# A column of maxima to all partitions: by a TensorE matmul, or by a VectorE transpose and two transfers through memory

## The chip, the cores and the metric

The kernel runs on one core of a Trainium2 chip. A core has a matrix engine (TensorE, PE in the profile, with PEld for its weight loads), three engines for elementwise work (VectorE as DVE, ScalarE as ACT, GpSimd as POOL), a queue engine that issues transfers (SyncE, SP), and DMA engines that move data between device memory and the on-chip memory SBUF. Matmuls write to PSUM, a small memory of banks. The metric is the device time of one execution in microseconds; lower is better.

## The reference

The inputs are q, k and v of shape (8 batches, 8 heads, 576 positions, 64 channels) and four weights. First comes a linear attention: q goes through a softmax over its 64 channels, k through a softmax over the 576 positions, then

```python
kv  = np.einsum('bhsd,bhse->bhde', k_s, v)      # 64x64 per head
out = np.einsum('bhsd,bhde->bhse', q_s, kv)
```

The heads are laid side by side (x has shape 8, 576, 512), and an MLP mixer follows:

```python
h  = np.maximum(xt @ w_tok1, 0.0) @ w_tok2      # xt: x transposed, over the positions
u  = x + h.transpose(0, 2, 1)
h2 = np.maximum(u @ w_ch1, 0.0) @ w_ch2         # 512 -> 1536 -> 512
return u + h2
```

The softmax of k needs, for every channel, the maximum over all positions. The division by its sum is done later, on the rows of kv.

## The kernel before

The work on q, k and v is cut into 32 **units**, one for each batch and pair of heads (4 units a batch). A unit's k lies in SBUF as `k_t`, with positions on the 128 partitions and five blocks of 128 channels in the free dimension (5 x 128 positions, two heads of 64 channels). The same k also comes transposed as `kt_t`, with the 128 channels on the partitions and the positions in the free dimension, so that the maximum is a reduction along the free dimension.

Units 0 to 7 (the "early" ones, L221 to L231) exponentiate the transposed copy and turn it back on TensorE. Units 8 to 31 go another way, L233 to L238. Their maxima `mc` are a column (128 partitions x 1), but they have to be subtracted from `k_t`, where the channels lie in the free dimension. So all 128 maxima must stand in every partition:

- L219, VectorE: `mc` is the maximum over `kt_t`.
- L233, ScalarE: `dg` is the identity scaled by `mc` per partition, that is a diagonal of the maxima.
- L235, TensorE: a matmul of a matrix of ones with `dg` gives a PSUM bank in which every row holds all maxima.
- L236, ScalarE: that bank is copied to `mb` in SBUF.
- L237, GpSimd: `mb` is subtracted from `k_t`. L238, ScalarE: the exponential.

`dg` and `mb` are single buffers; `mc` has two; `kt_t` has one buffer for the later units and `k_t`, `q_t` have two.

What follows for a unit: `softmax_q` (L245 to L267, with the split of q into a high and a low part, the low part by GpSimd, L115), `stage_kv` (the matmuls of `k_t` with v, L277), `stage_y` (L337), `stage_qT` (transposes of q on VectorE, L315 and L323), `stage_h1` (L345) and `stage_u` (L381). Their PSUM banks come in turn from the four of the pool `ps_h`.

Around this runs the channel MLP as 108 **steps**, nine groups of 512 columns by twelve blocks of the hidden dimension. Step (g, f) does `ch1` (L409, twelve matmuls into a `ps_h` bank), then ScalarE and VectorE make `h2h` and `h2l` from it (L412, L413), and `ch2` (L421, twelve matmuls into four `ps_o` banks) consumes them; `ch2` of a step stands behind `ch1` of the next one in the program. Every third step takes the stages of one unit between its `ch1` and `ch2`, from the table `todo` that is written out by hand.

In that table the softmax of unit n+1 stands at the same step as the matmuls of unit n, and the loads of unit n+2 half a step later. All loads go through SP's queue: `kt_t`, `q_t` and `k_t` by L137, L140 and L144, v by L154 and L155. The results go out through ScalarE's queue (L454). Each engine and each queue works through its own instructions in order. That order, in which work of later units may stand ahead of earlier program text, is settled when the kernel is built, by a scheduler that works with estimated durations; on the chip it is fixed, and an instruction whose input is late holds up what is behind it on its engine.

Of the kernel before, what the change touches and what calls it, by code (L numbers as in the profile page):

```python
# [8 lines left out]
F32 = mybir.dt.float32  # L9
F32R = mybir.dt.float32r  # L10
U32 = mybir.dt.uint32
AF = mybir.ActivationFunctionType
# [3 lines left out]
P = 128  # L16
# [4 lines left out]
def attn_mixer_kernel(ctx: ExitStack, tc: tile.TileContext, q, k, kt, v, wt, out, dims):  # L21
# [3 lines left out]
    nc = tc.nc  # L25
    B, H, S, D, TOK, DM, DCH, wide = dims
    NJ = DM // P
# [8 lines left out]
    NE = 2 * NJ  # L36
# [6 lines left out]
    sm = ctx.enter_context(tc.tile_pool(name="sm", bufs=2))  # L43
# [6 lines left out]
    ident = const.tile([P, P], F32R, name="ident")  # L50
# [11 lines left out]
    ones = const.tile([P, P], F32, name="ones")  # L62
# [26 lines left out]
    dg = lay.tile([P, P], F32, name="dg")  # L89
    for i in range(3):  # L90
        slots[i][1] = lay.tile([P, NJ, CW], F32R, name=f"ul{i}")
    mb = lay.tile([P, P], F32, name="mb")
# [14 lines left out]
    Q = 32  # L107

    def f32(ap):
        return ap.bitcast(F32)  # L110
# [8 lines left out]
    def ps_unit(dtype=F32):  # L119

        pools = unit_banks[0]
        pool, name = pools[turn[0] % len(pools)]
        turn[0] += 1
        return pool.tile([P, 512], dtype, name=name)
# [87 lines left out]


    turned_k = []

    def softmax_k(u):
        ktt = u["kt"]
        mc = sm.tile([P, 1], F32, name="mc")
        nc.vector.tensor_reduce(mc, ktt, axis=AX.X, op=ALU.max)  # L219
        kx = u["k"]  # L220
        if u["early"]:  # L221
            nc.vector.tensor_scalar(mc, mc, -1.0, None, op0=ALU.mult)
            nc.scalar.activation(ktt, ktt, AF.Exp, bias=mc)
            t = ps_unit()
            for c in range(C):
                nc.tensor.transpose(t[:, c * P : (c + 1) * P], ktt[:, c * P : (c + 1) * P], f32(ident))
            nc.scalar.copy(kx[:, 0:C, :], t.rearrange("p (c d) -> p c d", c=C))
            t = ps_unit()
            turned_k.append(nc.tensor.transpose(t[:, 0:P], ktt[:, S0 : S0 + P], f32(ident)).ins)
            nc.scalar.copy(kx[:, C, :], t[:, 0:P])  # L230
            return  # L231

        nc.scalar.activation(dg, f32(ident), AF.Copy, scale=mc)  # L233
        t = ps_unit()
        nc.tensor.matmul(t[:, 0:P], ones, dg, start=True, stop=True)  # L235
        nc.scalar.copy(mb, t[:, 0:P])  # L236
        nc.gpsimd.tensor_tensor(kx, kx, mb.unsqueeze(1).broadcast_to([P, C1, P]), op=ALU.subtract)  # L237
        nc.scalar.activation(kx, kx, AF.Exp)  # L238

# [223 lines left out]
    def soft(n):  # L463
        if n < NU:
            softmax_k(units[n])
            softmax_q(units[n])
# [204 lines left out]
```

## Time and profile before

| | before |
|---|---|
| runs shown, median (lowest to highest) | 818.27 us (816.95 to 819.36) |
| the profiled execution's own time | 817.88 us |
| its span in the trace | 816.1 us |
| granted TensorE clock, mean | 0.992 of full speed |
| DVE busy, ACT busy, POOL busy | 486.7 us, 342.2 us, 83.6 us |
| instructions | 11997 |

The profile is one execution. The span runs from the first to the last recorded instruction; the time of the execution is 1.8 us longer than it. A matmul is recorded with its whole way through the array, so that the records of neighbouring matmuls overlap; how long one holds the array is read from the distance between their starts, or from the chain of work, in which each piece begins where the one before it ends. A 32-bit matmul of `ones` with `dg` leaves two records. Five line numbers serve for many tiles: L114 and L115 are the two instructions of the helper `split`.

### The profile page before, as it was taken

To read this page: it belongs to the slowest core of one execution; us is meant where nothing else is said; L and a number is where in the kernel's file an instruction comes from. 1 tells how busy PE (TensorE), PEld (TensorE's weight loads), DVE (VectorE), ACT (ScalarE), POOL (GpSimd) and SP (SyncE) were. 2 spreads that over 40 slices of the span, in tenths; PEclk is the share of its full clock that TensorE was granted. 3 is DMA by queue.
4 is the path that set the end of the run, shared out by engine and by line. 5 is a ranking of instruction groups with operands and counts; after the bars stand their busy time and mean duration, and the time that the engine had idled before them with its cause. 6 is when DMAs were issued, how large, how long until landed. Compare 5 with 4: busy or idle time off the path is not lost.

```text
span 816.1 us, 11997 instructions
## 1 busy us (share of the span) xinstructions
PE 797.1 (98%) x4512; PEld 677.0 (83%) x4512; DVE 486.7 (60%) x1104; ACT 342.2 (42%) x898; POOL 83.6 (10%) x69
## 2 busy tenths in 40 slices
PE   7799999989999999999999999999999999999997
PEld 5688888878888888888888888888888888888886
DVE  6999998887876555755576555755575314113112
ACT  6977564448553334343444444443443321101110
POOL 1000010102121100111111111111011100000200
PEclk8999999999999999999999999999999999999999
DMA  9752433414223111322232222312121001001001
GB/s 298 245 162 93 149 110 109 145 65 124 86 63 115 52 30 53 110 61 64 63 100 79 64 64 63 113 51 63 26 87 35 15 1 51 1 1 52 1 1 51
DMA packets 60633, 63.55 MB, mean 78 GB/s; under 512 B 40864, under 2 KB 40992, under 8 KB 60576
## 3 DMA queue, kind: packets, MB, share of 16 engines
q1 hardware_dynamic: 55392, 53.36, 21.8%
q10 hardware_dynamic: 5184, 9.44, 3.1%
q8 instruction: 35, 0.57, 0.3%
q14 instruction: 22, 0.18, 0.1%
HBM read 53.35 MB, written 9.44 MB: 77 GB/s over the span
## 4 chain that ended last, share of the span: by engine, by line
PE 89%; DVE 6%; DMA 3%; ACT 1%; issue 1%; DVEq 0%; ACTq 0%
PE ps_h L409 34%; PE ps_o L421 34%; PE ps_h L381 8%; PE ps_h L337 6%; PE ps_h L277 2%; DMA stg<-in_w 2%; PE ps_h L345 1%; PE ps_o L381 1%; DVE mc L219 1%; PE ps_h L235 1%; DVE cv_s L176 1%; DVE q_t L323 1%; DMA q_t<-in_q 1%; DVE st L245 1%; ACT q_t L251 1%
## 5 line engine op out<-in xcount | busy, mean ns | idle before, releaser
L409 PE MATMUL ps_h<-uh,cw 128*128 128x512 f32 x864 | 269.7, 392 | 0.6 <-DVE cw L115 0.6
L421 PE MATMUL ps_o<-h2h,cw 128*128 128x512 f32 x864 | 263.4, 394 | 2.2 <-DVE cw L115 2.2
L421 PEld LDWEIGHTS ps_o<-h2h,cw 128*128 128x128 f32 x864 | 160.6, 189 | 34.3 <-ACT h2h L412 2.4
L409 PEld LDWEIGHTS ps_h<-uh,cw 128*128 128x128 f32 x864 | 160.3, 188 | 33.2 <-DVE cw L115 1.0
L412 ACT ACTIVATE h2h<-ps_h 128x512 fp32r<-128x512 f32 x108 | 64.5, 597 | 292.8 <-PE ps_h L409 276.6
L413 DVE SCALAR_TENSOR_TENSOR h2l<-ps_h,h2h 128x512 fp32r<-128x512 f32 x108 | 74.0, 685 | 187.3 <-ACT h2h L412 186.9
L409 PE MATMUL ps_h<-ul,cw 128*128 128x512 f32 x432 | 168.2, 389 | 0.0
L421 PE MATMUL ps_o<-h2l,cw 128*128 128x512 f32 x432 | 161.7, 392 | 0.0
L421 PEld LDWEIGHTS ps_o<-h2l,cw 128*128 128x128 f32 x432 | 81.4, 189 | 16.8
L409 PEld LDWEIGHTS ps_h<-ul,cw 128*128 128x128 f32 x432 | 81.1, 188 | 17.0
L115 POOL TENSOR_TENSOR ql<-q_t,qh 128x640 fp32r<-128x640 f32 x24 | 39.3, 1636 | 484.8 <-ACT qh L114 406.3
L323 DVE COPY q_t<-cv_s 32x160 f32<-32x160 f32 (+1 forms) x264 | 65.8, 249 | 6.3 <-POOL ql L115 3.0
L245 DVE TENSOR_REDUCE st<-q_t 128x10 f32<-128x640 f32 x32 | 26.2, 818 | 41.8 <-DMA q_t<-in_q 41.8
L237 POOL TENSOR_TENSOR k_t<-k_t,mb 128x640 f32<-128x640 f32 x24 | 38.0, 1582 | 73.8 <-ACT mb L236 73.8
L323 ACT COPY q_t<-cv_s 32x128 f32<-32x128 f32 (+1 forms) x120 | 36.8, 307 | 2.1 <-DVE cv_s L315 0.7
L219 DVE TENSOR_REDUCE mc<-kt_t 128x1 f32<-128x640 f32 x32 | 26.0, 812 | 14.7 <-ACT dg L233 12.4
L381 PE MATMUL ps_h<-w2h,hh 128*128 128x320 f32 (+1 forms) x112 | 33.4, 299 | 0.0
L256 ACT ACTIVATE q_t<-q_t 128x640 f32<-128x640 f32 x24 | 17.8, 741 | 36.4 <-DVE q_t L255 36.4
L381 PE MATMUL ps_h<-w2l,hh 128*128 128x320 f32 (+1 forms) x112 | 33.0, 296 | 0.0
L381 PE MATMUL ps_h<-w2h,hl 128*128 128x320 f32 (+1 forms) x112 | 32.7, 298 | 0.0
L388 ACT CAST uh<-ps_h 128x320 fp32r<-128x320 f32 (+4 forms) x76 | 25.4, 336 | 15.1 <-PE ps_h L381 11.8
L389 DVE TENSOR_TENSOR ul<-ps_h,uh 128x320 fp32r<-128x320 f32 (+4 forms) x76 | 27.2, 373 | 4.0 <-ACT uh L388 3.1
(144 smaller groups left out, 1061.9 us busy)
## 6 DMA issues: line engine op xcount, KB each, us to landing
stg<-in_w SPq DMA_DIRECT2D x28, 512.0 KB, 4.1
kt_t<-in_kt SPq DMA_DIRECT2D x32, 320.0 KB, 3.1
q_t<-in_q SPq DMA_DIRECT2D x32, 320.0 KB, 3.3
v_t<-in_v SPq DMA_DIRECT2D x64, 128.0 KB, 2.8
out<-stg ACTq DMA_DIRECT2D x32, 256.0 KB, 2.1
k_t<-in_k SPq DMA_DIRECT2D x24, 320.0 KB, 3.5
v_t<-in_v SPq DMA_DIRECT2D x32, 32.0 KB, 2.7
out<-part ACTq DMA_DIRECT2D x4, 256.0 KB, 2.0
```

What stands on the lines that cost most here:

```text
L115: lo_eng.tensor_tensor(lo, src, f32(hi), op=ALU.subtract)
L219: nc.vector.tensor_reduce(mc, ktt, axis=AX.X, op=ALU.max)
L237: nc.gpsimd.tensor_tensor(kx, kx, mb.unsqueeze(1).broadcast_to([P, C1, P]), op=ALU.subtract)
L245: nc.vector.tensor_reduce(st[:, 0, :], qt, axis=AX.X, op=ALU.max)
L323: eng(qx[ys, 0:n, xs], turned[xs, 0:n, ys])
L337: nc.tensor.matmul(y[:, 0:TOK], a, w, start=(i == 0), stop=(i == len(mm) - 1))
L381: nc.tensor.matmul(t[:, 0:N], a, w, start=(i == 0), stop=(i == len(mm) - 1))
L389: nc.vector.tensor_tensor(ul, src, f32(uh), op=ALU.subtract).ins,
L409: nc.tensor.matmul(t, cw[f][x][:, n, :], w, start=(i == 0), stop=(i == 3 * NJ - 1))
L412: nc.scalar.activation(hh, t, AF.Relu).ins,
L413: nc.vector.scalar_tensor_tensor(hl, t, 0.0, f32(hh), op0=ALU.max, op1=ALU.subtract).ins,
L421: nc.tensor.matmul(o, cw[f][x][:, n, :], w, start=(first and i == 0), stop=(last and i == 2))
```

## The change

For the last twenty units (`u["n"] >= NE + NJ`, units 12 to 31), L233, L235 and L236 are replaced. The maximum goes straight into the first column of `dg`. One VectorE transpose of 32 x 32 blocks turns columns 0 to 31 of `dg` into columns 32 to 63, block by block: in partition 0, 32, 64 and 96 there then stands a row of 32 maxima. (Columns 1 to 31 hold older values, which land in other rows and aren't read.) One transfer on SP's queue brings the four rows to a tile `row` of 128 numbers in device memory, which has two buffers; a second transfer on the same queue reads it into all 128 partitions of `mb`. L237 and L238 stay as they are. Units 8 to 11 keep the matmul.

```diff
+    dram = ctx.enter_context(tc.tile_pool(name="dram", bufs=2, space=bass.MemoryType.DRAM))
 
     def softmax_k(u):
         ktt = u["kt"]
-        mc = sm.tile([P, 1], F32, name="mc")
+        through = u["n"] >= NE + NJ
+        mc = dg[:, 0:1] if through else sm.tile([P, 1], F32, name="mc")
         nc.vector.tensor_reduce(mc, ktt, axis=AX.X, op=ALU.max)
...
-        nc.scalar.activation(dg, f32(ident), AF.Copy, scale=mc)
-        t = ps_unit()
-        nc.tensor.matmul(t[:, 0:P], ones, dg, start=True, stop=True)
-        nc.scalar.copy(mb, t[:, 0:P])
+        if through:
+
+            nc.vector.transpose(dg[:, Q : 2 * Q], dg[:, 0:Q])
+            row = dram.tile([P // Q, Q], F32, name="row")
+            nc.sync.dma_start(row, dg[0:P:Q, Q : 2 * Q])
+            nc.sync.dma_start(mb, row.rearrange("(o x) q -> o (x q)", o=1).broadcast_to([P, P]))
+        else:
+            nc.scalar.activation(dg, f32(ident), AF.Copy, scale=mc)
+            t = ps_unit()
+            nc.tensor.matmul(t[:, 0:P], ones, dg, start=True, stop=True)
+            nc.scalar.copy(mb, t[:, 0:P])
         nc.gpsimd.tensor_tensor(kx, kx, mb.unsqueeze(1).broadcast_to([P, C1, P]), op=ALU.subtract)
         nc.scalar.activation(kx, kx, AF.Exp)
```

## The prediction, made before the result was known

> **What bounds the kernel now.** I read the busy shares first, then busy time by stretches, then the chain of work that ended last. The engine shares of the page:
>
> ```profile
> PE 797.1 (98%) x4512; PEld 677.0 (83%) x4512; DVE 486.7 (60%) x1104; ACT 342.2 (42%) x898; POOL 83.6 (10%) x69
> ```
>
> An average hides stages, so the same by stretches (length, then PE, PEld, DVE, ACT and POOL busy, clock, DMA share, GB/s):
>
> ```profile
> 140.00:190.00 50.00, 46.78 (x254) 38.76 (x253) 41.60 (x89) 25.62 (x72) 6.55 (x4) 0.97 0.37 115
> 190.00:240.00 50.00, 50.00 (x320) 43.21 (x319) 38.90 (x97) 30.00 (x88) 8.20 (x6) 1.00 0.25 71
> ...
> 300.00:400.00 100.00, 100.00 (x604) 85.98 (x602) 61.10 (x146) 44.50 (x107) 15.47 (x10) 1.00 0.25 75
> ...
> 600.00:700.00 100.00, 100.00 (x548) 85.07 (x547) 41.09 (x92) 27.34 (x65) 6.19 (x4) 1.00 0.11 34
> ```
>
> From 190 us on TensorE has no gap: 100.00 of 100.00 us, at full clock, while VectorE has 39 us in 100 free and ScalarE 55. A busy array alone could still mean matmuls that stretch for another reason, so I look at what one costs. The chain of work over two neighbouring units (start, length, engine, tile, line, instructions):
>
> ```profile
> 410.77 0.73 PE ps_h L277 x20
> 411.50 1.85 PE ps_h L337 x14
> 413.35 0.22 PE ps_h L235 x2
> 413.57 2.76 PE ps_o L421 x12
> 416.33 2.72 PE ps_h L409 x12
> ...
> 422.21 2.74 PE ps_h L409 x12
> 424.95 0.68 PE ps_o L421 x3
> ...
> 432.76 0.73 PE ps_h L277 x20
> 433.50 1.85 PE ps_h L337 x14
> 435.35 1.39 PE ps_o L421 x6
> 436.74 0.22 PE ps_h L235 x2
> 436.96 1.39 PE ps_o L421 x6
> ```
>
> Everything on the chain is PE, each piece begins where the last ended, and one unit's period is 22.0 us (432.76 less 410.77). A full-width matmul takes 2.72 / 12 = 0.227 us wherever it stands. So TensorE's own instruction stream sets the time here, and a matmul taken out of it should shorten the span by its slot.
>
> [...]
>
> **The change part by part.** *Taken from TensorE.* One line's instructions (duration min/median/max in ns, first and last start), and its first and last place in the chain among the units concerned:
>
> ```profile
> L235 PEld LDWEIGHTS ps_h<-dg,ones x48: 186/188/189, 145.5 to 635.1; 128*128 128x128 f32 x48
> L235 PE MATMUL ps_h<-dg,ones x48: 270/273/377, 145.7 to 635.2; 128*128 128x128 f32 x48
> ```
>
> ```profile
> 216.54 0.22 PE ps_h L235 x2
> ...
> 635.29 0.22 PE ps_h L235 x2
> ```
>
> 48 records are 24 units of two; the four units that keep the matmul have the first four places, so the twenty that lose it run from 216.54 to 635.29 us, all in the stretch without gaps. The slot is 0.22 us in the chain. Where L235 stands inside a run of L421 (eleven units: 216.54 and from 436.74 on, and they read like the second piece above) there is a little more: 1.39 + 0.22 + 1.39 = 3.00 us against 2.75 for the twelve L421 undivided after L337, so 0.25. Where it stands ahead of the run (nine units) it is 0.22 to 0.23, since the 2.76 stays. Sum: 11 x 0.25 + 9 x 0.23 = 4.8 us. The bounds are 20 x 0.22 = 4.4 us from below and 20 x 2 x 0.273 = 10.9 us from above (whole durations, as if nothing overlapped); the chain is the nearer, so I take 4.8 and keep 5.5 as the upper end, since start to start is what the neighbours wait for.
>
> [...]
>
> *Taken from ScalarE, added to VectorE.* The groups (busy, mean ns, idle before and its cause), and nearest for the new transpose:
>
> ```profile
> L233 ACT ACTIVATE dg<-ident,mc 128x128 f32<-128x128 f32 x24 | 9.8, 408 | 0.2
> ```
>
> ```profile
> L236 ACT COPY mb<-ps_h 128x128 f32<-128x128 f32 x24 | 6.4, 265 | 9.4 <-PE ps_h L235 9.3
> ```
>
> ```profile
> L315 DVE STREAM_TRANSPOSE cv_s<-q_t 128x640 f32<-128x640 f32 x24 | 20.1, 839 | 0.3
> ...
> L282 DVE TENSOR_SCALAR rs<-ps_h 128x1 f32<-128x1 f32 x27 | 4.0, 150 | 0.1
> ```
>
> ScalarE loses 20 x (0.408 + 0.265) = 13.5 us and waits for L235. A transpose of 128x32 lies between 0.15 us (L282, almost no data) and 0.84 us (128x640); by its size it is near the first, so 0.2 us, 4 us in all (3 to 17). Neither engine sets the time, so I put both at zero for the end. The freed `ps_h` bank is worth nothing for the same reason: TensorE doesn't wait for a bank. VectorE's reduction now writes into the single `dg`, which the next unit may overwrite only when the first transfer has read it; that is over long before the next reduction, 22 us on.
>
> *Added to SP's queue and the DMA engines.* No 512-byte transfer to memory and no 64 KB broadcast is in the trace. The nearest rows (size, median us from issue to landing):
>
> ```profile
> out<-stg ACTq DMA_DIRECT2D x32, 256.0 KB, 2.1
> ...
> v_t<-in_v SPq DMA_DIRECT2D x32, 32.0 KB, 2.7
> ```
>
> Sizes of 32 to 256 KB hardly differ, so for small ones I take 2.1 us out and 2.7 us in: 4.8 us. SP must see the first landed before it issues the second, and issues for about 0.3 to 0.6 us each, so some 6 us from the transposed rows to `mb`; as bounds 3 us and 8 us. The DMA engines are at a quarter of their time, and 20 x 64 KB is 1.3 MB on top of 63.55 MB.
>
> What covers these 6 us? SP's queue in one period:
>
> ```profile
> 413.13 0.55 SPq L140 DMA_DIRECT2D q_t<-in_q  x1
> 413.72 0.42 SPq L144 DMA_DIRECT2D k_t<-in_k  x1
> 415.74 0.33 SPq L137 DMA_DIRECT2D kt_t<-in_kt  x1
> 433.40 0.93 SPq L154 DMA_DIRECT2D v_t<-in_v  x2
> ```
>
> and the reduction on VectorE, the subtraction on GpSimd, and the exponential with its neighbour on ScalarE:
>
> ```profile
> 414.89 0.82 DVE L219 TENSOR_REDUCE mc<-kt_t 128x1 f32<-128x640 f32 x1 [1.44 <-ACT dg L233]
> ```
>
> ```profile
> 414.52 1.57 POOL L115 TENSOR_TENSOR ql<-q_t,qh 128x640 fp32r<-128x640 f32 x1 [18.90 <-ACT qh L114]
> 416.05 1.56 POOL L237 TENSOR_TENSOR k_t<-k_t,mb 128x640 f32<-128x640 f32 x1
> ```
>
> ```profile
> 414.44 0.41 ACT L233 ACTIVATE dg<-ident,mc 128x128 f32<-128x128 f32 x1
> ...
> 418.04 0.74 ACT L238 ACTIVATE k_t<-k_t 128x640 f32<-128x640 f32 x1
> 419.09 0.60 ACT L412 ACTIVATE h2h<-ps_h 128x512 fp32r<-128x512 f32 x1 [0.31 <-PE ps_h L409]
> ```
>
> Two covers. First, `dg` written at 414.44 is used by the L235 at 436.74: the column lies 22 us until TensorE reaches its matmul, where the new way needs 6. Second, `k_t` exponentiated at 418.04 to 418.78 is read by L277 at 432.76, 14 us later. Between 416.1 and 433.4 SP has nothing to issue, so the two transfers fit there. Behind SP's new wait stand the next v loads, which wait for TensorE at 432.76 anyhow, and `kt_t`, `q_t`, `k_t` of units more than a period ahead. `mb` has one buffer: the second transfer waits for L237 of the unit before, done at 417.6. Behind L237 on GpSimd stands only the low part of q (one other instruction per period), and behind L238 on ScalarE stands L412.
>
> **Sum:** 4.8 us off, nothing added: span 816.1 to 811.3 us, execution 817.88 to **813.1 us** (the median of the runs shown, 818.27, would come to 813.5).
>
> **The rivals.**
>
> *ScalarE held by the transfers (slower).* The order on the engines is fixed with estimated durations, and the trace has one place where a transfer lands later than the order allowed for:
>
> ```profile
> DVE st L245 <- DMA q_t<-in_q: 41.8, 22, 3.2
> ```
>
> VectorE sits 1.9 us on average, 3.2 at most, before L245. If L238 (or L237 ahead of it) is placed as if `mb` were there at once, ScalarE stands still and L412 behind it is late. How much is free? L412 starts at 419.09 and takes 0.60, L413 behind it about 0.7; the L421 that needs both starts at 424.95. So 424.95 - 419.09 - 1.3 = 4.6 us are free, and each microsecond beyond costs one per unit. With 1.9 us late there is no loss; with the whole chain of 6 us unforeseen it is 1.4 us a unit, 28 us, less 4.8: 841 us. The point of decision is 4.6 + 0.24 us of lateness. Against it: both covers above. Chance 0.10, and it would mostly be a milder one, 820 to 841.
>
> *Nothing gained.* Another order comes out of the scheduler, and small waits of TensorE take what was freed: 0.24 us a unit suffices, and since SP, GpSimd and ScalarE all get their instructions in another order, q's path (L245 to L323, which already waits for its load) or L267 behind the low part of q may come later than now. Against it: PE doesn't wait once for them now. 817.9 us, chance 0.15, between 815.4 and 820.3.
>
> *More than forecast.* If weight loads were what fills TensorE, each L235 pair would give back its two loads of 188 ns: 817.88 - 7.5 = 810.4 us, chance 0.03. [...]
>
> **How the numbers follow.** A measurement of this kernel tells about 0.3% from no change, that is 2.5 us, or 815.4 us. The forecast has 0.72, with its own range 812.4 (5.5 us) to 815.4 us (half the gain given back to new waits). Faster: 0.72 + 0.03 = 0.75; same 0.15; slower 0.10. From 812.0 to 817.4 us there lie the forecast and about half of the second rival, 0.8 together.
>
> **What would show it.** Right: 8 matmul records at L235's line instead of 48 (PE count 4512 less 40 in both columns), PE still without gaps from 190 to 700 us, a period per unit of about 21.75 us, L237 no longer waiting for ScalarE but for a DMA, both new transfers landing within 2 to 3.5 us each, and SP with idle time left. Wrong: waits of PE on `h2h` or `h2l`, a wait of ScalarE's L238 above 4.6 us, L277 waiting for `k_t`, or a period of 22 us with fewer matmuls in it.

## The result, and the profile after

The changed kernel is **slower**: 829.91 us (median of 4 runs, 829.06 to 831.16) against 818.09 us for the kernel before beside it (816.95 to 819.36), a ratio of 1.0151 with a 95% interval of 1.0137 to 1.0165. The prediction of 813.1 us, with a range up to 817.4, was wrong in its sign. The profiled execution took 830.42 us with a span of 828.6 us. Lines have moved by two to nine: L219 is now L221, L237 is L246, L277 is L286, L345 is L354, L413 is L422; the new transpose is L237 and the two transfers are L239 and L240.

Page of the changed kernel, busy shares, then the shares of the chain of work that ended last, then the row of the second transfer (size, median us from issue to landing):

```profile
PE 800.2 (97%) x4472; PEld 675.3 (81%) x4472; DVE 506.4 (61%) x1124; ACT 328.5 (40%) x858; POOL 84.9 (10%) x69
...
PE 70%; DVE 15%; DMA 9%; ACT 2%; issue 2%; SPq 1%; POOL 0%; DVEq 0%; POOLq 0%; ACTq 0%
...
mb<-row SPq DMA_DIRECT2D x20, 64.0 KB, 2.8
```

The forty records of L235 are gone, as the change says (4512 to 4472), and a transfer lands in 2.8 us. But TensorE is now followed on only 70% of the chain, and VectorE and transfers stand on 24% of it. In the kernel before it was 89% and 9%:

```profile
PE 89%; DVE 6%; DMA 3%; ACT 1%; issue 1%; DVEq 0%; ACTq 0%
```

Busy time by stretches of the changed kernel (columns as in the prediction) says where:

```profile
190.00:240.00 50.00, 45.82 (x274) 38.90 (x273) 36.72 (x92) 25.88 (x73) 10.01 (x6) 1.00 0.33 96
240.00:300.00 60.00, 55.05 (x317) 46.42 (x316) 44.21 (x95) 19.99 (x47) 7.38 (x5) 0.94 0.43 128
300.00:400.00 100.00, 99.97 (x573) 84.73 (x571) 64.03 (x143) 39.61 (x92) 14.72 (x10) 1.00 0.18 53
...
600.00:700.00 100.00, 100.00 (x571) 85.31 (x570) 48.31 (x111) 31.20 (x77) 7.82 (x5) 1.00 0.13 41
```

Before, 190 to 240 us was full (50.00); now 4.2 us are missing there and 5.0 in the next 60 us, where the DMA share is 0.43 and the clock 0.94. From 300 us on TensorE has almost no gap (0.8 us in all from 300 to 700 us). The same is seen in when each unit's matmuls with v begin (L277, now L286; us from the span's start, read from TensorE's timeline):

| unit | before | after | after less before |
|---|---|---|---|
| 8 | 156.90 | 157.63 | +0.73 |
| 11 | 215.31 | 218.66 | +3.35 |
| 12 | 235.61 | 241.26 | +5.65 |
| 13 | 256.70 | 263.01 | +6.31 |
| 14 | 278.70 | 290.75 | +12.05 |
| 15 | 300.71 | 313.97 | +13.26 |
| 16 | 322.72 | 335.89 | +13.17 |
| 31 | 653.05 | 665.60 | +12.55 |

I call the last column the **arrears** below. Nearly all of them are made between 185 and 315 us; over the next fifteen units only 0.6 us is won back, where the forecast's 0.24 us a unit would have given 3.6.

What happens in that stretch is in the rows of the tile `dg` in the changed kernel, with that of the second transfer (count, duration min/median/max in ns, first and last start in us), beside the row of the same reduction in the kernel before:

```profile
L221 DVE TENSOR_REDUCE dg<-kt_t x20: 807/820/822, 202.4 to 295.0; 128x1 f32<-128x640 f32 x20
L237 DVE STREAM_TRANSPOSE dg<-dg x20: 169/207/214, 205.5 to 296.8; 128x32 f32<-128x32 f32 x20
L239 SPq DMA_DIRECT2D row<-dg x20: 487/495/612, 205.8 to 297.4; - x20
L240 SPq DMA_DIRECT2D mb<-row x20: 326/327/334, 207.8 to 609.1; - x20
```

```profile
L219 DVE TENSOR_REDUCE mc<-kt_t x32: 762/814/822, 3.9 to 571.2; 128x1 f32<-128x640 f32 x32
```

All twenty maxima are taken within 92.6 us (202.4 to 295.0), one every 4.9 us, not one per period of 22. Before, a maximum lay in one of two buffers `mc` until ScalarE had read it, ScalarE wrote the single `dg` only after TensorE's matmul of the unit before had read it, and that matmul stood in TensorE's stream: VectorE could be three units ahead of TensorE's L235 and no more (the maximum of unit 24 starts at 414.89, after the L235 of unit 21 at 413.35). The change took that brake away. `dg` is free as soon as the first transfer has read it, so the order made at build time pulls all later units' maxima, transposes, transfers to memory and loads of `kt_t` into the stretch after unit 12. The rows are all written by 297.9 us but read until 609.1, and at most fourteen later rows are written before a row is read. The two buffers of `row` are thus no brake: as built, each of the twenty rows has a place of its own in device memory.

What stands behind these pieces on VectorE and on SP's queue had to wait (2.71 us on VectorE, and 5.29 us on SP's queue where it was 0.71 before, in the two places shown here). VectorE's timeline (start, length; in brackets the idle time before and what ended it) and SP's, both of the changed kernel:

```profile
262.42 0.82 DVE L221 TENSOR_REDUCE dg<-kt_t 128x1 f32<-128x640 f32 x1 [1.11 <-DMA kt_t<-in_kt]
263.27 0.21 DVE L237 STREAM_TRANSPOSE dg<-dg 128x32 f32<-128x32 f32 x1
266.19 0.82 DVE L221 TENSOR_REDUCE dg<-kt_t 128x1 f32<-128x640 f32 x1 [2.71 <-DMA kt_t<-in_kt]
266.93 0.68 DVE L422 SCALAR_TENSOR_TENSOR h2l<-ps_h,h2h 128x512 fp32r<-128x512 f32 x1
```

```profile
259.11 0.34 SPq L137 DMA_DIRECT2D kt_t<-in_kt  x1
260.76 0.49 SPq L239 DMA_DIRECT2D row<-dg  x1
263.27 0.33 SPq L137 DMA_DIRECT2D kt_t<-in_kt  x1
263.69 0.49 SPq L239 DMA_DIRECT2D row<-dg  x1
267.04 0.34 SPq L137 DMA_DIRECT2D kt_t<-in_kt  x1
267.76 0.49 SPq L239 DMA_DIRECT2D row<-dg  x1
268.30 0.98 SPq L154 DMA_DIRECT2D v_t<-in_v  x2
```

The low part `h2l`, which TensorE needs for its next `ch2` and which reads a `ps_h` bank that TensorE is to write again, stands behind a maximum that waits 2.71 us for its own load. The load of v stands behind three pairs of load and transfer: it leaves at 268.30, 5.29 us after the matmuls that free its buffer began (263.01). In the kernel before, the same load follows those matmuls (256.70) by 0.71 us:

```profile
257.41 0.93 SPq L154 DMA_DIRECT2D v_t<-in_v  x2
```

TensorE's own waits in the changed kernel from 180 us on (tile and line that waited, what for; total us, times, longest; the largest four of seven):

```profile
PE ps_h L346 <- DVE h2l L422: 4.5, 2, 3.4
PE ps_o L430 <- ACT h2h L421: 2.3, 2, 1.6
PE ps_h L390 <- ACT hh L361: 1.7, 2, 1.2
PE ps_h L390 <- DVE hl L362: 1.7, 1, 1.7
```

The longest is that one `h2l`. L346 reads nothing that `h2l` writes, so what it waits for is the bank. It costs more than its 3.43 us, as TensorE's timeline and the stretches of 4 us around it show (columns as above; the seventh figure, after POOL's count, is the granted clock):

```profile
267.67 0.58 PE L346 MATMUL ps_h<-w1h,qh 128*128 128x256 f32 x1 [3.43 <-DVE h2l L422]
...
268.48 0.41 PE L346 MATMUL ps_h<-w1h,qh 128*128 128x256 f32 x1
268.69 0.41 PE L346 MATMUL ps_h<-w1l,qh 128*128 128x256 f32 x1
```

```profile
264.00:268.00 4.00, 0.57 (x2) 0.34 (x2) 1.81 (x4) 0.00 (x0) 0.00 (x0) 0.74 0.29 82
268.00:272.00 4.00, 4.00 (x17) 3.81 (x17) 2.23 (x7) 0.98 (x3) 0.00 (x0) 0.50 0.63 163
272.00:276.00 4.00, 4.00 (x17) 3.25 (x17) 2.97 (x3) 2.40 (x8) 2.75 (x2) 0.91 0.77 245
```

After the gap the clock is 0.50 for 4 us and 0.91 in the next 4: 2.0 + 0.4 = 2.4 us of full speed are lost. Gap and clock together are 5.8 us, and unit 14 begins 27.74 us after unit 13 where it was 22.00 before: 5.74 more. The clock was low after some shorter gaps too: in g_free16 (a run below) it was 0.57 after one of 2.25 us.

```profile
304.08 0.39 PE L346 MATMUL ps_h<-w1h,qh 128*128 128x256 f32 x1 [2.25 <-DVE h2l L422]
```

```profile
304.00:308.00 4.00, 3.92 (x17) 3.73 (x18) 1.71 (x5) 0.00 (x0) 0.00 (x0) 0.57 0.29 86
```

After gaps shorter still it was not low: in the changed kernel the clock over the next 4 us was 1.00 after gaps of 1.58 us (to 192.32) and 1.68 us (to 236.32).

### The profile page after: what moved, and what is told of

Read it like the earlier page. It is cut to its first block, busy times and chain, and to the rows that moved or that the text cites. A ratio compares the mean times of both kernels' runs of the same rounds, so it can differ in the third digit from the quotient of the medians.

```text
span 828.6 us, 11964 instructions
## 1 busy us (share of the span) xinstructions
PE 800.2 (97%) x4472; PEld 675.3 (81%) x4472; DVE 506.4 (61%) x1124; ACT 328.5 (40%) x858; POOL 84.9 (10%) x69
## 4 chain that ended last, share of the span: by engine, by line
PE 70%; DVE 15%; DMA 9%; ACT 2%; issue 2%; SPq 1%; POOL 0%; DVEq 0%; POOLq 0%; ACTq 0%
PE ps_h L418 27%; PE ps_o L430 26%; PE ps_h L390 7%; PE ps_h L346 5%; DMA kt_t<-in_kt 4%; DVE q_t L332 4%; DMA q_t<-in_q 3%; PE ps_h L286 2%; DMA stg<-in_w 2%; DVE st L254 1%; PE ps_o L390 1%; PE ps_h L354 1%; DVE dg L221 1%; DVE h2l L422 1%; DVE q_t L264 1%
## 5 line engine op out<-in xcount | busy, mean ns | idle before, releaser
L422 DVE SCALAR_TENSOR_TENSOR h2l<-ps_h,h2h 128x512 fp32r<-128x512 f32 x108 | 73.3, 678 | 155.6 <-ACT h2h L421 155.6
L430 PE MATMUL ps_o<-h2l,cw 128*128 128x512 f32 x432 | 163.5, 394 | 0.8 <-DVE h2l L422 0.6
L332 DVE COPY q_t<-cv_s 32x160 f32<-32x160 f32 (+1 forms) x264 | 82.2, 312 | 7.5 <-POOL ql L115 4.2
L115 POOL TENSOR_TENSOR ql<-q_t,qh 128x640 fp32r<-128x640 f32 x24 | 39.7, 1654 | 457.3 <-ACT qh L114 434.6
L246 POOL TENSOR_TENSOR k_t<-k_t,mb 128x640 f32<-128x640 f32 x24 | 38.1, 1586 | 111.3 <-ACT mb L245 62.0
L346 PE MATMUL ps_h<-w1h,qh 128*128 128x256 f32 x96 | 29.7, 309 | 4.5 <-DVE h2l L422 4.5
L247 ACT ACTIVATE k_t<-k_t 128x640 f32<-128x640 f32 x24 | 17.7, 739 | 33.5 <-POOL k_t L246 33.5
```

Source lines behind the costliest of these rows:

```text
L115: lo_eng.tensor_tensor(lo, src, f32(hi), op=ALU.subtract)
L332: eng(qx[ys, 0:n, xs], turned[xs, 0:n, ys])
L346: nc.tensor.matmul(y[:, 0:TOK], a, w, start=(i == 0), stop=(i == len(mm) - 1))
L422: nc.vector.scalar_tensor_tensor(hl, t, 0.0, f32(hh), op0=ALU.max, op1=ALU.subtract).ins,
L430: nc.tensor.matmul(o, cw[f][x][:, n, :], w, start=(first and i == 0), stop=(last and i == 2))
```

## The experiments

Two theories stood at first. **The bunch**: the removed matmul is worth what was forecast, and the loss comes from twenty units' maxima and transfers running ahead. **The rival, ScalarE held**: each unit is late for its transfers, as named in the prediction. Later runs ask which part of the bunch costs. Medians, the ratio to the kernel before measured beside each with its 95% interval, and the arrears at units 11, 15 and 31, read as in the table above:

| kernel | median us | ratio | arrears 11 / 15 / 31 |
|---|---|---|---|
| the change | 829.91 | 1.0151 (1.0137 to 1.0165) | 3.35 / 13.26 / 12.55 |
| a_held | 816.84 | 0.9989 (0.9974 to 1.0003) | 2.51 / 1.71 / -1.68 |
| b_ahead | 824.85 | 1.0087 (1.0060 to 1.0114) | 5.08 / 6.86 / 6.86 |
| c_twice | 821.20 | 1.0043 (1.0028 to 1.0058) | -1.15 / -0.24 / 3.33 |
| e_both | 816.99 | 0.9993 (0.9980 to 1.0007) | 1.90 / 2.17 / -0.76 |
| f_held16 | 815.23 | 0.9962 (0.9948 to 0.9975) | 0.81 / 0.81 / -2.55 |
| g_free16 | 828.20 | 1.0122 (1.0097 to 1.0147) | 0.32 / 0.32 / 11.84 |
| i_rows | 822.59 | 1.0057 (1.0041 to 1.0072) | 4.48 / 5.11 / 5.66 |
| d_tail | 828.38 | 1.0123 (1.0108 to 1.0138) | 3.36 / 14.85 / 11.12 |
| s_rows_tail | 815.50 | 0.9969 (0.9954 to 0.9983) | 1.68 / 1.14 / -2.59 |
| j_ahead_rows_held | 825.62 | 1.0096 (1.0083 to 1.0109) | 5.75 / 10.46 / 6.85 |
| k_noload | 827.31 | 1.0110 (1.0086 to 1.0134) | 3.25 / 10.45 / 9.95 |
| p_narrow | 826.21 | 1.0104 (1.0075 to 1.0132) | 3.87 / 9.91 / 8.51 |
| q_norows | 822.14 | 1.0057 (1.0039 to 1.0075) | 3.81 / 5.92 / 4.57 |
| r_norows_tail | 819.74 | 1.0026 (1.0016 to 1.0035) | 2.61 / 3.88 / 0.15 |
| t_norows_narrow | 819.61 | 1.0022 (1.0012 to 1.0032) | 1.10 / 0.49 / -1.16 |

Arrears come from one profiled execution, and up to 1.4 us of them are there already at unit 8, ahead of everything that was changed (1.8 and 2.4 in b_ahead and j_ahead_rows_held, whose maxima run ahead from 152 us on). t_norows_narrow's profiled execution (817.18 us) was the fastest of its ten, so its arrears flatter it by some 2 us.

### a_held: the change, with each maximum held to its period

```diff
+    scaled = []
...
-        nc.vector.tensor_reduce(mc, ktt, axis=AX.X, op=ALU.max)
+        with behind(scaled if through else []):
+            nc.vector.tensor_reduce(mc, ktt, axis=AX.X, op=ALU.max)
...
-        nc.vector.reciprocal(rs, rs)
+        scaled[:] = [nc.vector.reciprocal(rs, rs).ins]
```

`behind` orders the maximum after the previous unit's division by its sum.

> The changed kernel with one thing added: the maximum of a later unit is ordered on VectorE behind the reciprocal of the unit before it, so that it can no longer run ahead. Theory 1 (the loss is made between 190 and 315 us, where VectorE takes the maxima of all twenty units at once, each behind a load into the single kt buffer; 12 to 13 us by the positions of L277): that loss goes, 829.9 - 13 = 817 us or a little less, with 20 maxima spread from 200 to 620 us. Theory 2 (the loss is made in every unit by the transfers, the late subtraction and the exponential that wait for them): still 827 to 830 us.

The same reduction in a_held:

```profile
L223 DVE TENSOR_REDUCE dg<-kt_t x20: 799/800/803, 218.9 to 631.1; 128x1 f32<-128x640 f32 x20
```

With one maximum per period the 13 us are gone, with every part of the change still there. From unit 16 to 31 the arrears fall from 1.50 to -1.68, that is 0.21 us a unit: the freed slot of the matmul. The bunch is the cause of the loss, and a_held comes out where the first theory put it (817 us). What it left open are the 1.3 us that are added between units 8 and 11 and keep this kernel level with the one before.

### b_ahead: the kernel before, with its maxima let run ahead

```diff
+    mcs = const.tile([P, 20], F32, name="mcs")
...
-        mc = sm.tile([P, 1], F32, name="mc")
+        n = u["n"]
+        mc = sm.tile([P, 1], F32, name="mc") if n < NE + NJ else mcs[:, n - NE - NJ : n - NE - NJ + 1]
```

> The kernel before, with the matmul, but each later unit's maximum in a column of its own, so that the reductions can run ahead as they do in the changed kernel. Theory 1: running ahead alone costs some 10 us, 828 us or more, without any transfer through memory. Theory 2: about as before, 817 to 819 us.

This has TensorE's matmul and no transfers; only the two buffers of `mc` became twenty. It lost 0.87%. So a removed brake alone costs 7.1 us (824.85 less 817.77), without anything that the change added. That is less than the 10 us and more that were expected of it.

### c_twice: the kernel before, with the matmul issued twice

```diff
+        if u["n"] >= NE + NJ:
+            nc.tensor.matmul(t[:, 0:P], ones, dg, start=True, stop=True)
```

> The kernel before with the matmul of ones and dg issued twice for the last twenty units. If its slot in TensorE's stream is worth 0.22 to 0.25 us, as the chain shows, 818.1 + 4.4 to 5.0 = 822.5 to 823.1 us. If the slot is hidden in some other limit, 818 us, and the predicted gain of 4.8 us was never there.

821.20 us beside 817.77 is 3.4 us for twenty matmuls, below the 4.4 to 5.0 expected. But the profiled execution has 1.15 us less than the kernel before at unit 11, ahead of the first doubled matmul; between units 11 and 31 the arrears grow by 4.48, or 0.224 us each. By that the slot was sized right.

### e_both: a_held, with the subtraction held too

On top of a_held, L246 is ordered behind GpSimd's part of the split of q of its own unit:

```diff
+            if n >= NE + NJ:
+                with behind(low[-1:]):
+                    less_max(units[n])
```

(`less_max` holds L246 and L247; `low` collects GpSimd's L115.)

> As a_held, and the subtraction and the exponential of a unit are ordered behind the low part of the same unit's q on GpSimd, a period later than in the changed kernel, so that they no longer wait for the load of k_t. Theory 1 alone: as a_held. If what is left per unit (a copy of VectorE that lasts 1.6 instead of 0.25 us beside the subtraction, and h2l late by some tenths) comes from that place of the subtraction: 3 to 4 us less than a_held, 813 to 814 us, faster than before.

Nothing came of it. GpSimd's timeline of a_held shows why: there the subtraction stands behind L115 in any case, and waits for its transfer.

```profile
262.60 1.56 POOL L115 TENSOR_TENSOR ql<-q_t,qh 128x640 fp32r<-128x640 f32 x1 [13.69 <-ACT qh L114]
267.95 1.56 POOL L248 TENSOR_TENSOR k_t<-k_t,mb 128x640 f32<-128x640 f32 x1 [3.79 <-DMA mb<-row]
```

### f_held16 and g_free16: the new way from unit 16 on, held and not held

```diff
-        through = u["n"] >= NE + NJ
+        through = u["n"] >= NE + 2 * NJ
```

f_held16 has a_held's edit as well; g_free16 has this line alone.

> a_held, with the new way from unit 16 on instead of unit 12 (sixteen units; units 8 to 15 keep the matmul). In a_held the period is 0.21 us shorter per unit from unit 12 on, but its unit 11 already stands 2.5 us behind before. If that arrears comes from another order around the changeover at 140 to 215 us, starting where TensorE has no gaps avoids it: 817.8 - 16 x 0.21 = 814.4 us. If the arrears belongs to the new way wherever it begins, about 817 us.

> The changed kernel with the new way from unit 16 on and nothing held (f_held16 without its hold). If the hold is what makes f_held16 815.2, sixteen maxima taken ahead cost again: 818 - 3.4 + 16/20 x 16 = 827 us. If it was the place of the changeover, it is near f_held16, 815 to 817 us.

f_held16 is **faster than both kernels**, 815.23 us, between its two expected values and nearer the first. g_free16 loses nearly as much as the change itself, and its loss has moved with the units: its arrears stand at 0.32 at unit 15 and are 5.76, 10.00 and 13.62 at 16, 17 and 18. Stretches of g_free16, then of f_held16:

```profile
240.00:300.00 60.00, 60.00 (x338) 51.44 (x337) 37.77 (x88) 23.63 (x58) 10.87 (x7) 1.00 0.24 74
300.00:400.00 100.00, 91.06 (x507) 77.56 (x506) 65.08 (x144) 33.60 (x80) 12.50 (x8) 0.95 0.32 91
```

```profile
240.00:300.00 60.00, 60.00 (x336) 51.33 (x336) 34.70 (x81) 23.50 (x57) 9.30 (x6) 1.00 0.19 56
300.00:400.00 100.00, 100.00 (x600) 85.91 (x599) 62.72 (x151) 40.16 (x95) 16.99 (x10) 1.00 0.27 79
```

The 60 us that were short of work in the change are full in g_free16, and its hole of 8.9 us lies one stretch later. So the loss belongs to the bunch, not to what else runs at 250 us, as expected of this run (827 us).

### i_rows, d_tail and s_rows_tail: the transfers in order, the subtraction in order, and both

i_rows orders each first transfer behind the second transfer of the unit before; d_tail is e_both's edit without a_held's; s_rows_tail has both. All three compute everything.

```diff
+    spread = []
...
-            nc.sync.dma_start(row, dg[0:P:Q, Q : 2 * Q])
-            nc.sync.dma_start(mb, row.rearrange("(o x) q -> o (x q)", o=1).broadcast_to([P, P]))
+            with behind(spread):
+                nc.sync.dma_start(row, dg[0:P:Q, Q : 2 * Q])
+            spread[:] = [nc.sync.dma_start(mb, row.rearrange("(o x) q -> o (x q)", o=1).broadcast_to([P, P])).ins]
```

> The changed kernel with one ordering added on SP's queue: the transfer of a unit's rows to memory stands behind the transfer of the unit before it into mb. The maxima stay free, and can be ahead only by the few units that dg and the row transfer let through (five are taken early instead of twenty). Theory 1 (it is the bulk of twenty maxima and kt loads in 200 to 300 us that costs): 815 to 818 us, as a_held. If any maximum taken early costs its share, 829.9 - 15/20 x 13 = 820 us.

> The changed kernel with only the subtraction and the exponential of a unit ordered behind the low part of the same unit's q on GpSimd, a period later; the maxima run ahead as they do. In the changed kernel units 16 to 31 gain 0.7 us on before where a_held gains 3.2. If the early subtraction, which waits for k_t and stands beside VectorE's copies, is what eats that: 829.9 - 2.5 = 827.4 us. If not: 829 to 830 us.

> The whole computation: row transfers held behind the previous unit's spread (as in i_rows, 822.6 us) and the subtraction held behind its own unit's q split (as in d_tail). If the two parts add up, i_rows loses the 3 us of d_tail over units 16 to 31 and nothing of the arrears at unit 15: 819 to 820.5 us. If the subtraction is also behind the arrears that are made before unit 15: 815 to 818 us.

Time over the kernel before, from the medians of the same batch:

| | subtraction free | subtraction held |
|---|---|---|
| transfers free | +11.8 (the change) | +10.4 (d_tail) |
| transfers held | +4.6 (i_rows) | -2.2 (s_rows_tail) |

i_rows and d_tail came out at none of their expected values, s_rows_tail at the second of its two. Holding the subtraction is worth 1.4 us while the transfers bunch, and 6.8 us once they don't. The two do not add: alone they are worth 7.2 and 1.4 us, together 14.0. That TensorE, made late by the one, hides the other is the likely reason; no run shows it by itself. With both held, the whole loss is gone and the kernel is 0.31% faster than before, though no maximum is held by itself. The order of the transfers is a brake on them as well, since `dg` is free only when its transfer has read it: in s_rows_tail twenty maxima take 352.6 us (201.5 to 554.1).

```profile
L225 DVE TENSOR_REDUCE dg<-kt_t x20: 807/810/821, 201.5 to 554.1; 128x1 f32<-128x640 f32 x20
```

How an early subtraction costs time is seen in one period of i_rows, on VectorE and on GpSimd, and then in s_rows_tail on VectorE (the copies are the last step of turning q):

```profile
445.57 3.96 DVE L334 COPY q_t<-cv_s 32x160 f32<-32x160 f32 x11
```

```profile
445.83 1.64 POOL L248 TENSOR_TENSOR k_t<-k_t,mb 128x640 f32<-128x640 f32 x1 [0.74 <-DMA k_t<-in_k]
```

```profile
439.97 2.71 DVE L342 COPY q_t<-cv_s 32x160 f32<-32x160 f32 x11
```

In i_rows GpSimd subtracts from a `k_t` that has just landed, during VectorE's copies, and these take 1.25 us longer. Their groups in the kernel before, in the change and in s_rows_tail (busy, mean ns, idle before):

```profile
L323 DVE COPY q_t<-cv_s 32x160 f32<-32x160 f32 x144 | 39.5, 274 | 4.7 <-POOL ql L115 3.0
```

```profile
L332 DVE COPY q_t<-cv_s 32x160 f32<-32x160 f32 x144 | 55.9, 388 | 5.9 <-POOL ql L115 4.2
```

```profile
L342 DVE COPY q_t<-cv_s 32x160 f32<-32x160 f32 x144 | 38.8, 269 | 5.2 <-POOL ql L116 3.6
```

The change made 144 copies 16.4 us dearer, without any change to them. One by one in its trace: the 113 copies beside no subtraction take 249 ns on average, 255 at most; the 31 that overlap one take 896 on average, and the longest, 1.64 us, lasts as long as a subtraction. Holding the subtraction takes that back. It also gives d_tail its better second half: 3.7 us won from unit 15 to 31, where the change won 0.7.

### j_ahead_rows_held: maxima ahead in columns of their own, the rest in its period

```diff
+    mcs = const.tile([P, 20], F32, name="mcs")
...
-            nc.vector.transpose(dg[:, Q : 2 * Q], dg[:, 0:Q])
+            with behind(scaled):
+                nc.vector.tensor_copy(dg[:, 0:1], mc)
+                nc.vector.transpose(dg[:, Q : 2 * Q], dg[:, 0:Q])
```

> The changed kernel with its maxima in columns of their own, free to run ahead as in b_ahead, while a copy of the column into dg, the transpose and the two transfers are ordered behind the reciprocal of the unit before, as in a_held. If the cost of running ahead is that of the maxima and kt loads alone: b_ahead's 7.1 us less the 4.2 us of twenty slots, 817.8 + 2.9 = 820.7 us. If the changed kernel's larger loss needs the transposes and row transfers ahead too, this stands well below its 829.9; if not, at about 829.

It came out between what the two theories gave. Its arrears at unit 15 are larger than b_ahead's (10.46 against 6.86), and 3.6 us are won back by unit 31, 0.23 a unit. Holding the transfers while the maxima and their loads bunch takes back 4.2 of the 11.8 us and leaves 7.6; to lose nothing, the maxima must be kept back too.

### k_noload, p_narrow, q_norows, r_norows_tail, t_norows_narrow: parts of the bunch taken out

```diff
+        if n > NE + NJ:
+            u["kt"] = units[NE + NJ]["kt"]
+        else:
```

k_noload has this edit: no load of the transposed k after unit 12. The four others have it too. p_narrow adds the first line below, q_norows leaves out both transfers, r_norows_tail is q_norows with d_tail's edit, t_norows_narrow is q_norows with p_narrow's.

```diff
-        nc.vector.tensor_reduce(mc, ktt, axis=AX.X, op=ALU.max)
+        nc.vector.tensor_reduce(mc, ktt[:, 0:Q] if through else ktt, axis=AX.X, op=ALU.max)
...
-            row = dram.tile([P // Q, Q], F32, name="row")
-            nc.sync.dma_start(row, dg[0:P:Q, Q : 2 * Q])
-            nc.sync.dma_start(mb, row.rearrange("(o x) q -> o (x q)", o=1).broadcast_to([P, P]))
```

> The changed kernel without the loads of kt for units 13 to 31: their maxima are taken from unit 12's kt, so the output differs, but every maximum, transpose and transfer is still issued, and the twenty maxima still stand together in VectorE's order. If the loss of running ahead is VectorE standing in its order behind loads that land late (L221 waits for kt 12 times, and TensorE's longest gap, 3.4 us at 264 us, is behind one), it goes with the loads: 816 to 820 us. If it is VectorE's own time for twenty maxima and transposes (20 x 1.03 us in 95 us), it stays: 827 to 830 us.

> As k_noload (no loads of kt for units 13 to 31), and the maximum of units 12 to 31 is taken over the first 32 positions of 640 only. The order keeps its twenty maxima, transposes and row transfers together, but VectorE's time for a maximum falls from 0.82 to about 0.15 us. If VectorE's own work in that stretch is what delays h2l, hl and rs behind it, most of the loss goes: 815 to 819 us. If it is SP's queue (row transfers that wait for a transpose, with q's and v's loads behind them), it stays: 824 to 827 us.

> As k_noload, and both transfers of units 12 to 31 left out (mb keeps unit 11's maxima). Twenty maxima of full size and twenty transposes still stand together on VectorE; SP's queue holds only q, k and v. If VectorE's own work delays the rest: 824 to 827 us. If SP's queue does, with q's loads late behind waiting row transfers: 814 to 818 us.

> q_norows (no loads of transposed k after unit 12, no transfers of the maxima, so unit 11's maxima are subtracted throughout) with the subtraction of the maxima, and with it the exponential, held behind the GpSimd part of their own unit's q split. Median of q_norows 822.1 us. If the early subtraction and exponential make what is left of the loss there: 813 to 817 us, and units 16 to 31 gain 3 us or more against before. If the rest comes from VectorE's bunched maxima or from something not named yet: 819 to 822 us, with the arrears at unit 15 still near 5 us.

> q_norows (no loads of transposed k after unit 12, no transfers, unit 11's maxima kept) with each of the twenty maxima taken over 32 of 640 positions. SP's queue and VectorE's time are then both out of it at once. If VectorE's time makes the rest together with the queue: 815 to 818 us. If neither does: 821 to 823 us as q_norows, and the early subtraction is what is left.

I had taken the late loads of `kt_t`, for which VectorE waits before L221, to be the cause. That **fell**: without them k_noload is only 0.4% better than the change. p_narrow then takes nearly all of VectorE's time out of the maxima, and its medians give 1.0 us more, which is within the intervals; on its own VectorE's time isn't it either, and the time is in the range expected for SP's queue. Taking out the transfers is worth 5 us (827.31 to 822.14), which lies between the two ranges expected. SP's queue shows what stood behind them, here in the timeline of k_noload:

```profile
211.91 8.07 SPq L242 DMA_DIRECT2D row<-dg  x3
220.04 0.98 SPq L157 DMA_DIRECT2D v_t<-in_v  x2
221.07 1.32 SPq L158 DMA_DIRECT2D v_t<-in_v  x1
222.50 0.52 SPq L143 DMA_DIRECT2D q_t<-in_q  x1
```

Three row transfers hold the queue for 8 us, most of it until VectorE has turned their rows, and the loads of v and q stand behind. Without the transfers the other parts show: over the kernels before beside them, q_norows is at +4.9 us, with the subtraction held +2.1, with narrow maxima +1.9. r_norows_tail is in its second range, t_norows_narrow between its two. With the transfers in place the same narrowing gave 1.0 us (+10.0 to +9.0); without them it gives 3.0. That would be the pattern of the table of four above, but the intervals of k_noload and p_narrow reach 2 us either way, so it is not shown. Nor is it shown which of the loads behind the row transfers cost the 5 us. What the last 2 us of r_norows_tail and t_norows_narrow are stays open.

## Why the prediction was wrong

**The step that failed** is the one about the single buffer `dg`, in the part on VectorE: the first transfer's reading of it "is over long before the next reduction, 22 us on". It took the order of the kernel before as given and asked only whether the buffer would be late. It is never late; it is early, and by then nothing else holds the next reduction back. The next one came 4.9 us on, not 22. The same holds for the cover: "Between 416.1 and 433.4 SP has nothing to issue, so the two transfers fit there" counted one unit's transfers in one unit's gap; in SP's rows above, three units' loads and transfers stand ahead of one load of v. The facts for it were in the prediction: L219 waited for ScalarE's L233 (its quoted row says so), and ScalarE for TensorE's L235 (the row of L236: 9.3 us). "TensorE doesn't wait for a bank" went the same way: it held for the kernel before, and in the change the longest wait is for a bank. A removed instruction was priced by its time, and not by what waited for it.

**TensorE's slot** was right as a mechanism and at most a little high: 0.24 us a unit forecast, 0.21 in a_held and f_held16, 0.224 in c_twice, 0.23 in s_rows_tail (units 16 to 31), that is 4.2 to 4.7 us for twenty units where 4.8 was taken. f_held16 with sixteen units gets 2.8 us out of 3.4 (16 x 0.21). The 7.5 us of "More than forecast", two weight loads of 188 ns for each of twenty units, are not there: no run shows that weight loads fill TensorE, and the runs gave 0.21 to 0.23 us a unit where two loads would be 0.38.

**ScalarE and VectorE at zero for the end.** ScalarE's 13.5 us were indeed worth nothing. The transpose takes 0.207 us as estimated. But VectorE's place in the order was worth much more than its time, and a cost that was in no term was the subtraction's new place: GpSimd beside VectorE's copies. In i_rows the eleven copies lose 1.25 us beside a subtraction of 1.64; by what means GpSimd's work slows VectorE's is not shown. An early L237 thus had a price, and I did not weigh it.

**The transfers** were sized nearly right. The second lands in 2.8 us where 2.7 was taken; for the first the profile gives no landing time. From the end of the first new transpose (205.7) to the subtraction that waits for `mb` (211.04) it is 5.3 us where 6 were taken.

**The rivals.** "ScalarE held by the transfers" is not the mechanism. ScalarE's wait for the subtraction is at most 2.4 us, below the 4.6 us that the rival needed, and the arrears would have grown over all twenty units, where they grow over the first four:

```profile
ACT k_t L247 <- POOL k_t L246: 33.5, 21, 2.4
```

"Nothing gained" had the right cause in its first words, another order out of the scheduler, but gave it the size of what was freed. That an order can lose more than the edit's own terms had no place among the cases, so the range ended at 817.4.

**The signs.** Eight matmul records at L235's line: right. TensorE without gaps from 190 us on: wrong up to 300 us, nearly right after (0.8 us of gaps up to 700). A period of 21.75 us: 21.98 in the change (units 16 to 31), 21.81 in a_held and f_held16, 21.79 in s_rows_tail. Waits on `h2h` and `h2l`, named as a sign against, are what the trace shows. In s_rows_tail one line of them is left in the waits of TensorE from 180 us on:

```profile
PE ps_o L440 <- ACT h2h L431: 2.1, 2, 1.7
```

## What to carry to other kernels

Before an instruction or a buffer is taken out, ask what it held back: where a scheduler makes the order at build time, a producer that loses its brake can move far ahead, and the engines and queues that it shares fill up in front of work that is due now. Here the maxima came one every 4.9 us instead of one in 22, and one load of v left 5.29 us after the matmuls that free its buffer began, where it had been 0.71. Put the brake back by hand, here as an order behind a step of the unit before, and the loss is gone: 829.91 us became 816.84 with the maxima held and 815.50 with the transfers and the subtraction held; with sixteen units instead of twenty it was 815.23. Of the 4.8 us that were forecast, the kernels with twenty units gained 0.9 us (a_held) and 2.2 us (s_rows_tail). When several parts of such a bunch are each late enough, removing one can show little (here the subtraction held was worth 1.4 us alone, and 6.8 us with the transfers held too); test them in pairs before one is called harmless.

## What the hardware showed

- A gap of 3.43 us on TensorE was followed by a granted clock of 0.50 over 4 us: a matmul of 256 columns every 0.21 us (268.48 to 268.69), where the fourteen of L337 in the kernel before took 1.85 us, 0.13 each. The gap thus cost about 5.8 us. In g_free16 a gap of 2.25 us was followed by a clock of 0.57.
- VectorE copies that were not touched by the change took 388 ns on average against 274: 249 ns where GpSimd's subtraction did not overlap them, 896 where it did.
- A row of 0.5 KB to memory and a spread of 64 KB back cost little themselves (2.8 us to land for the second, and a_held, with all forty of them, is level with the kernel before); what they cost lay in the queue: in k_noload three of the first transfers held it for 8.07 us, most of that until their rows were there, with loads of v and q behind them, and without the transfers the kernel was 5 us faster.
